# Retention and a SwiGLU layer on one core: the sums of weight blocks are made in other units, kept in DRAM and read back for every unit

## The chip, the cores and the metric

The kernel runs on one core of a Trainium2 chip. The metric is the device time of one execution, in microseconds (us); lower is better. The kernel before took 670.7 us, the median of three runs (670.59 to 671.23).

The engines are named as in the profile: PE (TensorE, matmuls) with PEld (its weight loads), DVE (VectorE), ACT (ScalarE), POOL (GpSimd) and SP (SyncE, which here only issues DMAs). SBUF is the memory that the engines work on, PSUM the one that matmuls write to, DRAM the memory off the core.

## The reference: what is computed

Two layers, one after the other. The first is retention with a decay per head, in blocks of 64; the second is a SwiGLU layer after an RMS norm:

```python
intra = einsum('bhic,bhjc->bhij', qb, kb) * Dmask          # per block of 64
out[:, :, sl] = einsum('bhij,bhjd->bhid', intra, vb) + einsum('bhid,bhde->bhie', qb * lam_pow, kv_state)
kv_state = lam_block * kv_state + einsum('bhsd,bhse->bhde', kb * rev_pow, vb)

xn = x / sqrt(mean(x * x) + 1e-6) * rms_g                  # x: 3072 tokens x 512
g, val = xn @ w_gate, xn @ w_val                           # 512 x 1536 each
result = (g / (1 + exp(-g)) * val) @ w_out                 # 1536 x 512
```

Batch 4, 8 heads, 768 positions, head size 64: 3072 tokens of width 512. Everything is float32 at the kernel's borders.

## The kernel before

**Tiling.** The tokens are cut into six groups m = 0 to 5 of 512, the hidden width 1536 into twelve slices f = 0 to 11 of 128. A unit is one pair (m, f): the gate and the value product of that slice, the activation, and its share of the output product. There are 72 units, in the order m=0 with f=0..5, m=1 with f=0..11, m=0 with f=6..11 (units 0 to 23), and then m=2 to 5 with twelve slices each (units 24 to 71). Between the units run the retention products of a later group, as pairs of heads (`Pair`), and that group's norm (`Norm`).

**Precision.** Every operand of the large products is held as a float16 high part and a float16 rest (for the output product of the early units, as two parts in another 32-bit format). A product takes three passes: high by high, rest by high, high by rest.

**Two kinds of units.** Units 0 to 23 are classical: 12 matmuls of 128x512 for the gate, 12 for the value, 12 for the output. Units 24 to 71 (`strassen`) replace the eight half-size block products of gate and value by seven (`Product`, numbered 1 to 7), each of six 128x256 matmuls (L939). Products 3, 5, 6 and 7 read sums of weight blocks, and 5 to 7 sums of token blocks (`tx`) as their other operand. The output product takes 12 matmuls of 128x512 (L777 to L779).

**The sums of weight blocks** (`WeightSums`, one per slice f). The high part and rest of both weights are first added up (`whole`, two steps on POOL, L871); four steps on DVE form the four sums (`sums`, L886 to L890); each is then split into its float16 parts by copies on ACT (`high`, L904) and differences on POOL (`low`, L908). Where the result lies is told by `place`: the first two sums in the spare half of the tile of an output weight (`w16`), the third in memory that held the weights' squares (`col`) or a partial result (`partial`), the fourth over half of the gate weight of that slice itself. The last two can be written only when their places are no longer read. The sums of f = 0, 1 and 2 are due in units 18 to 20, those of 3 to 11 from unit 24.5 on, one per unit.

**Other work around them.** The weights arrive as raw 64-bit words on SP's queue and are converted in units up to 14 (`Weights`; TAKE). `Column` forms squares of each weight for bounds that unit 17 needs (`Norms`). `Halves` turns the output weights into float16 pairs once these bounds are known: f = 6 to 11 from unit 18.35 on, f = 0 to 5 from 24.5 on; each takes two steps on ACT (L268, L274), one on DVE (L277) and one on POOL (L282), with two of the three buffers of the tag "o". The same buffers serve the squares and the rows of the result.

**The order of the work.** Units 0 to 5 (`ramp`) are written out by hand. From unit 6 on, a planner (`Plan`) orders all steps: each has an engine, a cost in us, a due time in units, tiles that it reads and writes, and buffers that it opens. The planner walks through time, takes for each engine the step with the earliest due time that can start, and emits the instructions in that order. On the chip each engine then keeps this order. Loads of q, k and v ("LD"), of output weights ("LO") and stores ("ST") are engines of their own to the planner, but all of them go into the one queue of SP, which is served in order. A product step writes its PSUM bank: the "ps" tile for even units (`pp`), "pg" and "pv" for odd ones (`pa`, `pb`). A norm's factors (`spread`, `pr`, L658) take the "ps" tile too in m = 2 and 3.

## Time and profile before

| what | value |
|---|---|
| median of three runs | 670.7 us (670.59 to 671.23) |
| the profiled execution's own time | 672.56 us |
| its span, first to last instruction | 670.8 us |
| PE busy | 652.3 us, 97% |
| DVE busy | 428.0 us, 64% |
| ACT busy | 328.9 us, 49% |
| POOL busy | 160.1 us, 24% |
| DRAM traffic | 44.05 MB read, 6.29 MB written |
| granted TensorE clock | 0.998 |

How to read it: a row of waits names the instruction that stood idle, what released it, the total in us, the number of times and the longest. A row of lines gives line, engine, operation, tiles (out<-in), shapes, count, then busy us and the mean in ns, then the idle time ahead of it. A row of the timeline begins with the start in us from the span's beginning and the length in us; idle time ahead of it stands in brackets.

### The profile page before, as it was taken

The page shows a single profiled execution, that of the slowest core. Times are in us where ns is not written, and L with a number is a line of the kernel's source. Part 1 is how long each engine was busy: PE and PEld are TensorE (multiplying, and loading weights), DVE is VectorE, ACT ScalarE, POOL GpSimd, SP SyncE. Part 2 cuts the span into 40 slices and gives each one's busy share as a digit, 9 for nine tenths or more (in the row PEclk, how much of TensorE's full clock was granted, in tenths as well). Part 3 has the DMA queues.
Part 4 walks back from the last instruction along what each step waited for, and adds up shares of the span by engine and source line. Part 5 has one row for each costly group of instructions (what it writes and reads, how often), then busy time and mean ns, then how long its engine had stood idle before and what let it go on. Part 6 is the DMA issues. An engine that isn't in the chain of part 4 may idle for free.

```text
span 670.8 us, 12331 instructions
## 1 busy us (share of the span) xinstructions
PE 652.3 (97%) x5035; PEld 442.9 (66%) x5035; DVE 428.0 (64%) x779; ACT 328.9 (49%) x672; POOL 160.1 (24%) x144
## 2 busy tenths in 40 slices
PE   8999999999999999999979999999999999999997
PEld 8846665555656446777657777777777776767774
DVE  6798869876346887987875434477644377543333
ACT  3786558675324644564454443335444434433332
POOL 2300130012205844868822011001111001000000
PEclk9999999999999999999999999999999999999999
DMA  8966626311023001301100321100220000100001
GB/s 313 345 237 213 232 75 233 114 63 64 0 64 127 1 0 55 128 29 44 64 1 1 110 79 64 64 1 2 95 96 1 1 1 1 39 26 1 1 1 63
DMA packets 14312, 51.12 MB, mean 76 GB/s; under 512 B 1712, under 2 KB 1968, under 8 KB 12848
## 3 DMA queue, kind: packets, MB, share of 16 engines
q1 hardware_dynamic: 13968, 49.69, 20.9%
q8 instruction: 39, 0.64, 0.4%
q10 hardware_dynamic: 288, 0.66, 0.3%
q14 instruction: 17, 0.14, 0.1%
HBM read 44.05 MB, written 6.29 MB: 75 GB/s over the span
## 4 chain that ended last, share of the span: by engine, by line
PE 86%; DVE 8%; ACT 2%; POOL 1%; issue 1%; DMA 0%; DVEq 0%; ACTq 0%; POOLq 0%
PE pp L939 16%; PE pv L758 9%; PE acc L777 9%; PE pg L758 9%; PE pa L939 8%; PE acc L779 8%; PE acc L778 8%; PE pb L939 6%; PE pa L508 4%; PE po L569 3%; PE po L580 2%; PE pst L537 2%; DVE tx L990 1%; DVE ws L887 1%; ACT tx L986 1%
## 5 line engine op out<-in xcount | busy, mean ns | idle before, releaser
L779 PE MATMUL acc<-wo,hh 128*128 128x512 f16 (+1 forms) x288 | 110.3, 383 | 0.0
L778 PE MATMUL acc<-wo,hh 128*128 128x512 f16 (+1 forms) x288 | 110.2, 383 | 0.0
L777 PE MATMUL acc<-wo,hh 128*128 128x512 f16 x216 | 82.3, 381 | 0.2 <-DVE hh L1035 0.2
L939 PEld LDWEIGHTS <-wo 128*128 128x128 f16 x576 | 55.8, 98 | 30.1 <-issue 8.1
L939 PEld LDWEIGHTS <-wg 128*128 128x128 f16 x576 | 56.3, 98 | 19.4 <-issue 4.4
L758 PE MATMUL pg<-x,wg 128*128 128x512 f16 x288 | 67.8, 380 | 0.8 <-ACT sg L1010 0.5
L1028 ACT CAST hh<-sg 128x512 f16<-128x512 f32 (+1 forms) x72 | 44.4, 617 | 48.4 <-DVE sg L1017 23.5
L758 PE MATMUL pv<-x,wv 128*128 128x512 f16 x288 | 67.0, 379 | 0.0
L986 ACT COPY tx<-pp 128x256 f32<-128x256 f32 x72 | 26.8, 372 | 78.7 <-PE pp L939 76.3
L939 PEld LDWEIGHTS <-wv 128*128 128x128 f16 x576 | 56.2, 98 | 9.3 <-DVE xn L731 1.2
L528 POOL TENSOR_TENSOR qkv<-qkv,pw 128x512 f32<-128x512 f32 x22 | 28.4, 1291 | 106.2 <-PE pa L508 97.3
L990 DVE TENSOR_TENSOR tx<-pp,tx 128x256 f32<-128x256 f32 x48 | 20.3, 423 | 51.7 <-ACT sg L998 40.0
L986 ACT COPY tx<-pa 128x256 f32<-128x256 f32 x72 | 26.7, 371 | 48.7 <-PE pa L939 48.0
L758 PEld LDWEIGHTS <-wv 128*128 128x128 f16 x288 | 27.9, 98 | 33.6 <-issue 1.1
L758 PEld LDWEIGHTS <-wg 128*128 128x128 f16 x288 | 26.5, 98 | 34.7 <-issue 5.2
L1035 DVE TENSOR_TENSOR hh<-sg,hh 128x512 f16<-128x512 f32 x54 | 43.2, 800 | 5.1 <-ACT hh L1028 4.2
L939 PE MATMUL pp<-tx,wo 128*128 128x256 f16 x288 | 39.0, 272 | 3.9 <-DVE tx L990 3.1
L1004 DVE SCALAR_TENSOR_TENSOR sg<-tx,cv,sg 128x512 f32<-128x512 f32 x48 | 39.6, 825 | 4.1 <-DVE tx L990 0.5
L994 DVE TENSOR_TENSOR sg<-pp,tx 128x256 f32<-128x256 f32 x24 | 10.1, 423 | 45.5 <-ACT tx L986 43.5
L939 PE MATMUL pp<-x,wg 128*128 128x256 f16 x288 | 35.5, 272 | 3.1 <-DVE sg L994 2.6
L990 DVE TENSOR_TENSOR tx<-pb,tx 128x256 f32<-128x256 f32 x48 | 20.3, 424 | 27.9 <-PE pb L939 25.1
L779 PEld LDWEIGHTS <-hh 128*128 128x128 f16 x216 | 21.1, 98 | 25.5
(192 smaller groups left out, 1270.4 us busy)
## 6 DMA issues: line engine op xcount, KB each, us to landing
qkv<-in_qkv_dram SPq DMA_DIRECT2D x47, 512.0 KB, 4.8
raw_gv<-in_weights_dram SPq DMA_DIRECT2D x11, 1024.0 KB, 5.3
raw_o<-in_weights_dram SPq DMA_DIRECT2D x12, 512.0 KB, 4.4
out_dram<-o SPq DMA_DIRECT2D x23, 256.0 KB, 2.1
partial<-in_weights_dram SPq DMA_DIRECT2D x2, 512.0 KB, 11.4
qkv<-in_qkv_dram ACTq DMA_DIRECT2D x1, 512.0 KB, 4.0
out_dram<-o SPq DMA_DIRECT2D x1, 128.0 KB, 1.7
out_dram<-o ACTq DMA_DIRECT2D x1, 128.0 KB, 2.4
```

The costliest lines, as they stand in the source:

```text
L508: nc.tensor.matmul(self.pa[:, j, c, :], self.kT[r, c, :], self.qT[r, c, :], start=True, stop=True,)
L528: eng.tensor_mul(self.qT, self.qT, pw[:, p : p + 1, :].broadcast_to([P, GC, P]))
L758: nc.tensor.matmul(ps, w[:, kk, :], x[:, kk, :], start=i == kk == 0, stop=i == 2 and kk == NK - 1,)
L777: nc.tensor.matmul(acc, hl[:, ts_], oh, start=first, stop=False)
L778: nc.tensor.matmul(acc, hh[:, ts_], ol, start=False, stop=False)
L779: nc.tensor.matmul(acc, hh[:, ts_], oh, start=False, stop=last)
L939: nc.tensor.matmul(ps, w(ow, k), x(ox, k), start=first and i == k == 0, stop=i == 2 and k == 1, skip_group_check=True,)
L986: nc.scalar.copy(self.kept[:, i], self.pa)
L990: nc.vector.tensor_add(self.val[:, half], self.pb, self.kept[:, i])
L1004: nc.vector.scalar_tensor_tensor(self.sg, self.val, cv[:, self.f : self.f + 1], self.sg, ALU.mult, ALU.mult)
L1028: nc.scalar.copy(self.hh, self.sg)
L1035: nc.vector.tensor_sub(self.hl, self.sg, hh)
```

## The change

The sums of weight blocks no longer stay in SBUF. Each sum's float16 parts are formed in two buffers of the tag "o" and stored to DRAM as two blocks of 256 KB (`put`). Each of the units 24 to 71 reads the whole set of its slice back, 512 KB, into one of three buffers (`fetch`), the former places of output weights 8, 9 and 11, taken in turn. The fourth sum is read from there too, and no longer overwrites the gate weight.

Because no place has to become free, the sums of f = 0 to 5 can be made as soon as the weights are there: they are now due from unit 12.5 to 16.25, those of 6 to 11 from 24.8 to 30.3. A sum's splitting takes two copies on ACT and two differences on POOL, all of 128x512, instead of three each. The float16 output weights are put two to a tile (`PLACE`). The squares of the weights (`column_steps`) are due one unit earlier.

The planner has a fourth queue to order ("FE", the fetches, again on SP), adds 0.8 of the overlap to the cost of eight named kinds of DVE steps while POOL is busy (before: a quarter to every DVE step), looks 600 steps ahead instead of 420, and gets markers ("turn:...") that keep the users of the PSUM banks in the order of the units.

```diff
 class Halves: def high(self):
-            place = {HALF: NF, 0: NF - 1}.get(f, f - 1)
-            self.t = t = wpool.tile([P, 4, DM], F16, tag=f"wo{place}", name=f"wo16_{f}")
+            if f % 2 == 0:
+                w16[f] = w16[f + 1] = wpool.tile(
+                    [P, 2, 2, DM], F16, tag=f"wo{PLACE[f]}", name=f"wo16_{f}"
+                )
+            self.t = t = w16[f][:, f % 2]
...
+    PLACE = {6: 12, 8: 6, 10: 7, 0: 10, 2: 0, 4: 1}
+    STREAM = [8, 9, 11]
...
 class WeightSums:
+                self.t = stage.tile(
+                    [P, 2, 2, HG], F32, tag="raw_o", name=f"ws_{self.f}", bufs=2
+                )
             t = self.t
             if i == 0:
-                nc.vector.tensor_add(t[:, 0], g0, g1)
-                nc.vector.tensor_sub(t[:, 2], v0, g0)
+                nc.vector.tensor_add(t[:, 0, 0], g0, g1)
+                nc.vector.tensor_sub(t[:, 0, 1], v0, g0)
             else:
-                nc.vector.tensor_sub(t[:, 1], g1, t[:, 2])
-                nc.vector.tensor_sub(t[:, 3], v1, t[:, 1])
...
+                nc.vector.tensor_sub(t[:, 1, 0], g1, t[:, 0, 1])
+                nc.vector.tensor_sub(t[:, 1, 1], v1, t[:, 1, 0])
+
+        def high(self, i):
+            if i == 0:
+                self.o = {}
+            self.o[i] = o = op.tile([P, 2, 2, HG], F16, tag="o", name=f"s_{self.f}_{i}")
+            nc.scalar.copy(o[:, 0], self.t[:, i])
+
+        def low(self, i):
+            nc.gpsimd.tensor_sub(self.o[i][:, 1], self.t[:, i], self.o[i][:, 0])
+
+        def put(self, i):
             f = self.f
             if i == 0:
+                sums_dram[f] = dram.tile([P, 2, 2, 2, HG], F16, tag=f"sd{f}", name=f"sd_{f}")
+            nc.sync.dma_start(sums_dram[f][:, i], self.o[i])
+
+    def fetch(u, f):
+
+        t = wpool.tile(
+            [P, 2, 2, 2, HG], F16, tag=f"wo{STREAM[u % 3]}", name=f"ss_{u}"
+        )
+        nc.sync.dma_start(t, sums_dram[f])
+        streamed[u] = t
...
 class Product:
-                (raw(wg, 0), given(2, second)),
+                (summed(1, 1), given(2, second)),
                 (raw(wg, 2), given(0, second)),
-                (lambda o, k: pairs12[f][:, o, 0, cols[k]], lambda o, k: t[:, o, k, 0]),
-                (lambda o, k: pairs12[f][:, o, 1, cols[k]], lambda o, k: t[:, o, k, 1]),
-                (lambda o, k: s3[:, o, cols[k]], lambda o, k: t[:, o, k, 2]),
+                (summed(0, 0), lambda o, k: t[:, o, k, 0]),
+                (summed(1, 0), lambda o, k: t[:, o, k, 1]),
+                (summed(0, 1), lambda o, k: t[:, o, k, 2]),
...
 class Plan:
+        SHARED = (
+            "low", "mul_sums", "sums", "refine", "rest_high", "convert", "convert_o", "add_squares",
+        )
-        ENGINES = ("PE", "ACT", "DVE", "POOL", "LD", "LO", "ST")
+        ENGINES = ("PE", "ACT", "DVE", "POOL", "LD", "LO", "ST", "FE")
-        def run(self, horizon=1.3, reach=420):
+        def run(self, horizon=1.3, reach=600):
-                if eng == "DVE" and start < pool_until:
-                    cost *= 1.25
+                if eng == "DVE" and fn.__name__ in self.SHARED and start < pool_until:
+                    cost += 0.8 * min(cost, pool_until - start)
...
 def sum_steps(f, at):
+            step("POOL", 1.15, at + 0.1 * i, s.whole, i, r=[f"w{'vg'[i]}{f}"], w=[f"r{f}:{i}"],
+                 new=[] if i else [(f"r{f}", "a")])
         for i in range(2):
+            step("DVE", 0.84, at + 0.4 + 0.1 * i, s.sums, i, r=[f"r{f}:0", f"r{f}:1"], w=[f"ws{f}:{i}"],
+                 new=[] if i else [(f"ws{f}", "raw_o")])
+        for i in range(2):
+            step("ACT", 0.62, at + 0.6 + 0.1 * i, s.high, i, r=[f"ws{f}:{i}"], w=[f"so{f}{i}"],
+                 new=[(f"so{f}{i}", "o")])
+            step("POOL", 1.15, at + 0.7 + 0.1 * i, s.low, i, r=[f"ws{f}:{i}"], w=[f"so{f}{i}"])
+            step("ST", 0.05, at, s.put, i, r=[f"so{f}{i}"], w=[f"sd{f}:{i}"], lasts=4.0)
+
+    def fetch_steps(u, f):
+        step("FE", 1.5, 0, fetch, u, f, r=[f"sd{f}:0", f"sd{f}:1"], w=[f"ss{u}"],
+             new=[(f"ss{u}", f"wo{STREAM[u % 3]}")], lasts=4.0)
...
 def classical(u, h, norms=None):
-            w = [f"{name}{u}"]
+            w = [f"{name}{u}", f"turn:{name}"]
...
-                w.append("pc")
+                w += ["pc", "turn:pa"]
...
 def strassen(u, h):
+        fetch_steps(u, f)
+        s = f"ss{u}"
-        step("PE", cost, u, h.first, u, r=[v, *x01], w=[a], new=banks)
+        step("PE", cost, u, h.first, u, r=[v, *x01], w=[a, "turn:pg", "turn:pv"], new=banks)
...
-        step("PE", cost, u + 0.8, h.add, 3, r=[g, *x23], w=[b])
+        step("PE", cost, u + 0.8, h.add, 3, r=[s, *x23], w=[b])
...
-    SUMS = [(18, 18.6), (19, 19.6), (20, 20.3)]
-    SUMS += [(2 * NF, 2 * NF + 0.5 + 1.0 * (f - 3)) for f in range(3, NF)]
+    SUMS = [(12 if f < 5 else 16, 12.5 + 0.75 * f if f < 6 else 24.8 + 1.1 * (f - 6)) for f in range(NF)]
...
-                column_steps(f, u + 0.3)
+                column_steps(f, u - 0.7)
```

## The prediction

> **What bounds the kernel now.** I read the page first, then who TensorE (PE) waited for in stretches between unit ends, then the load of the other engines there.

> ```profile
> span 670.8 us, 12331 instructions
> ...
> PE 652.3 (97%) x5035; PEld 442.9 (66%) x5035; DVE 428.0 (64%) x779; ACT 328.9 (49%) x672; POOL 160.1 (24%) x144
> ...
> PE 86%; DVE 8%; ACT 2%; POOL 1%; issue 1%; DMA 0%; DVEq 0%; ACTq 0%; POOLq 0%
> ```

> PE is busy for 97% of the span and holds 86% of the chain that ended last. The change leaves the number of matmuls alone, so it can only win time in which PE stands still. The page puts that at 18.5 us (670.8 - 652.3), but it understates each stall, because a matmul's modelled end overlaps the next one:

> ```profile
> 595.73 0.38 PE L778 MATMUL acc<-wo,hh 128*128 128x512 f16 x1
> 595.95 0.38 PE L779 MATMUL acc<-wo,hh 128*128 128x512 f16 x1
> ```

> Starts are 0.22 apart and the recorded length is 0.38, so every listed wait hides another 0.16 us or so. Below, a stall costs its listed idle time plus 0.16.

> Group 2 (the twelve units of m=2, from the end of unit 23 at 254.5 to the end of unit 35 at 369) is where the waits gather. The waits of PE from 254 to 325, then from 325 to 369:

> ```profile
> PE pp L939 <- DVE sg L994: 1.8, 3, 0.7
> PE pp L939 <- DVE tx L990: 0.3, 1, 0.3
> PE pa L939 <- ACT tx L986: 0.2, 1, 0.2
> ```

> ```profile
> PE pp L939 <- ACT tx L986: 2.0, 3, 1.0
> PE pp L939 <- DVE xn L731: 0.9, 1, 0.9
> PE pp L939 <- DVE sg L994: 0.8, 2, 0.6
> PE pr L658 <- POOL y L649: 0.5, 1, 0.5
> ```

> First part: 2.3 + 5 x 0.16 = 3.1 us. Second part: 4.2 + 7 x 0.16 = 5.3 us. Together 8.4. The next group does the same products and the same kind of attention work with no weight sums, and loses 0.7 + 2 x 0.16 = 1.0 us in all (waits of PE from 369 to 471):

> ```profile
> PE pp L939 <- DVE tx L990: 0.7, 2, 0.3
> ```

> So about 7 us is the price of what group 2 does beside its products: nine of the twelve weight sums, and six of the twelve halvings of the output weights. The load of the engines in units 12 to 16, the two parts of group 2, and group 3 (columns: PE, PEld, DVE, ACT, POOL busy, clock, DMA share, GB/s):

> ```profile
> 138.70:179.00 40.30, 40.30 (x199) 22.25 (x198) 22.99 (x46) 21.95 (x40) 4.85 (x7) 1.00 0.08 28
> ...
> 254.50:325.00 70.50, 68.30 (x630) 49.09 (x627) 58.70 (x92) 38.33 (x86) 49.66 (x43) 1.00 0.23 76
> 325.00:369.00 44.00, 39.79 (x308) 28.43 (x306) 31.66 (x56) 21.52 (x49) 18.68 (x17) 1.00 0.01 1
> 369.00:470.80 101.80, 101.15 (x873) 73.40 (x872) 55.51 (x105) 43.83 (x96) 11.12 (x9) 1.00 0.15 53
> ```

> VectorE (DVE) is 83% busy in the first part and 55% in group 3; GpSimd (POOL) 70% against 11%. They are also in each other's way. The first three rows are DVE's sums from 254.5 to 325; the last is the same step over the whole kernel (min/median/max ns):

> ```profile
> L887 DVE TENSOR_TENSOR ws<-r 128x256 f32<-128x256 f32 x6 | 8.7, 1451 | 0.0
> ...
> L890 DVE TENSOR_TENSOR ws<-r,ws 128x256 f32<-128x256 f32 x6 | 5.2, 864 | 0.2
> L886 DVE TENSOR_TENSOR ws<-r 128x256 f32<-128x256 f32 x6 | 4.6, 767 | 1.3 <-POOL wg L908 1.2
> ...
> L889 DVE TENSOR_TENSOR ws<-r,ws 128x256 f32<-128x256 f32 x6 | 3.2, 536 | 0.0
> ```

> ```profile
> L887 DVE TENSOR_TENSOR ws<-r x12: 412/1372/1495, 196.0 to 354.0; 128x256 f32<-128x256 f32 x12
> ```

> One 128x256 step takes 0.41 us alone and up to 1.5 us beside GpSimd's; a sum's four cost 3.6 us (1.45 + 0.86 + 0.77 + 0.54) where 4 x 0.41 = 1.65 would do. The last sum's steps ran at 354, 15 us before the group's end: the sums trail through all of it.

> **The change part by part.**

> *PE's work: 0.* Seven products of six matmuls read the same shapes from another tile.

> *Sums 3 to 5 leave group 2, 6 to 11 stay (due 24.8 to 30.3).* In the first part six sums ran before (L887 x6) and six will run after. Per sum DVE has the same four steps; GpSimd has two halves of 512 instead of one of 512 and two of 256:

> ```profile
> L871 POOL TENSOR_TENSOR r<-wv 128x512 f32<-128x512 f16 x7 | 8.9, 1266 | 4.9 <-DVE ws L890 3.8 <-PE po L569 1.2
> L871 POOL TENSOR_TENSOR r<-wg 128x512 f32<-128x512 f16 x6 | 8.4, 1393 | 0.0
> ...
> L908 POOL TENSOR_TENSOR wo<-ws,wo 128x512 f16<-128x512 f32 x6 | 7.6, 1271 | 1.5 <-ACT wo L904 1.5
> L908 POOL TENSOR_TENSOR wg<-ws,wg 128x256 f16<-128x256 f32 x6 | 5.8, 969 | 0.2 <-ACT wg L904 0.2
> ```

> That is 1.27 + 1.39 + 1.27 + 2 x 0.97 = 5.9 us before and 1.27 + 1.39 + 2 x 1.27 = 5.2 after, too little to matter. So I leave the 3.1 us of the first part as they are (bounds: all of it gone, or 3.1 more). The second part loses its three sums. What stalls there is the norm of m=3 (unit 31): its spread sits in the PSUM bank that unit 32 needs until DVE has read it four times, the last read ending just before PE goes on:

> ```profile
> 336.34 0.74 DVE L731 SCALAR_TENSOR_TENSOR xn<-x,gs,pr 128x512 f32<-128x512 f32 x1
> ```

> ```profile
> 337.14 1.49 PE L939 MATMUL pp<-x,wv 128*128 128x256 f16 x12 [0.88 <-DVE xn L731]
> ```

> and then unit 32 runs alone, step by step, because the output products that would fill its gaps wait for DVE too. With DVE and GpSimd free of sums this should shrink to what the worst of the other hand-offs between groups costs, that before m=5 (waits of PE from 574 to 604):

> ```profile
> PE pp L939 <- DVE tx L990: 0.6, 2, 0.3
> PE pp L939 <- DVE x L719: 0.4, 1, 0.4
> PE pp L939 <- ACT tx L986: 0.3, 1, 0.3
> ```

> 1.3 + 4 x 0.16 = 1.9 us. So 5.3 - 1.9 = **3.4 us won** (bounds 0 and 5.3).

> *Sums 0 to 2 leave units 18 to 22.* There PE lost one stall, to the norm of m=2, and the sum of weight 2 is straight ahead of it on DVE:

> ```profile
> 232.17 0.43 DVE L890 TENSOR_TENSOR ws<-r,ws 128x256 f32<-128x256 f32 x1
> 232.51 0.68 DVE L609 TENSOR_TENSOR sq<-sq,sq 128x512 f32<-128x512 f32 x1
> ```

> ```profile
> PE pss L625 <- DVE sq L609: 0.8, 1, 0.8
> ```

> **1.0 us won** (0.8 + 0.16; bounds 0 and 1.0).

> *Sums 0 to 5 come into units 12 to 16.* PE is full there without a single wait, GpSimd is used for 4.9 of 40.3 us, DVE for 23.0. Six sums add 9.9 us to DVE at the step's lone time and 21.7 at the time beside GpSimd: 33 to 45 of 40.3. A unit there asks only two DVE steps of PE's path (gating and the low half), and both have the 12 gate matmuls (2.6 us at 0.22) before their bank is wanted. I take 0, the lower bound, because the nearest row is that of three sums in the equally classical units 18 to 21, which cost PE nothing but the norm's stall. The upper bound is the first part's 3.1 us, or 4.4 where DVE is overfull (45 - 40.3, rounded down; a rival below).

> [...]

> *The column work (square sums of the weights) moves one unit earlier:* into units 7 to 15, same steps; hidden behind PE's matmuls as before, 0. If that cover is gone it is the same rival.

> *24 stores and 48 loads are added on SyncE's queue.* A store is 256 KB and a load 512 KB in 4 KB rows; the nearest rows are the result's stores and the output weights' loads, with the latter's landing times min/median/max:

> ```profile
> out_dram<-o SPq DMA_DIRECT2D x23, 256.0 KB, 2.1
> ```

> ```profile
> DMA to landing us min/median/max: 3.6/4.4/9.4
> ```

> A load for unit u+3 is free to go after unit u's last use of its buffer, two units ahead. Two units take 14.8 us:

> ```profile
> 603.21 0.62 ACT L1028 CAST hh<-sg 128x512 f16<-128x512 f32 x1
> ```

> ```profile
> 618.05 0.62 ACT L1028 CAST hh<-sg 128x512 f16<-128x512 f32 x1
> ```

> Even the slowest landing, 9.4, leaves 5 us: 0 (upper bound below, as a rival). Traffic: 512 KB per 7.4 us is 71 GB/s above the 53 to 76 of the stretches above. A store waits for GpSimd's low half, and what stands behind it on the queue are q/k/v loads, the results' stores and the next loads of sums. A stall of a few us there is covered by the same 14.8 us; sums 6 to 11 are due about five units before their use.

> *Halvings keep their four instructions and only change place.* 0. They share three buffers with the stored sums, which now hold two of them until a store has landed. At 1.27 for the low half and 2.1 for the landing, six sums hold 6 x 2 x 3.4 = 41 of the 211 buffer-us (3 x 70.5) of the first part, so a halving rarely finds none.

> *The planner's new costs, turns and reach* change the order of everything after the ramp. It can add or take single stalls of 0.5 us: 0, plus or minus 1.5.

> **Sum:** -3.4 - 1.0 = -4.4 us. The profiled execution took 672.56 us, 1.76 around its span, so it would take 668.2. The median of the runs shown is 670.70, 1.86 below it; carried over, 666.3.

> **Rivals.**

> *Sums were DVE's whole trouble.* The sums' lower GpSimd load and a better order also clear the first part: 3.1 more, and the hand-off costs nothing: 1.9 more. 661.3. For it: group 3 loses only 1.0. Against: six sums and the halvings still run in that part, as densely as now.

> *The hand-off is the norm's own.* The bank is held by four reads in DVE's order whatever else runs; then only the 1.0 us goes: 669.7, no change. For it: three of its waits are on ScalarE copies in a chain inside one unit. Against: the hand-offs to m=4 and m=5 are cheap; but these norms take another way.

> *DVE overfull in units 12 to 16 (slower).* If a sum there costs DVE over 2.9 us ((40.3 - 23.0) / 6), weight 11 and the column sums come late and PE stands at unit 17, which needs both: 4.4 us. The same contention keeps sums 6 to 11 trailing into the norm of m=3, so that the 3.4 isn't won: 670.7 + 4.4 - 1.0 = 674.1. For it: the median of 1.37 us; against: the deadline is unit 17, and DVE has room in units 16 and 17.

> *A load of sums stuck behind a q/k/v load.* SyncE takes its queue in order, and it has stood on such loads for long:

> ```profile
> SPq L86 <- PE po L580: 228.9, 11, 53.2
> ```

> Nothing waited behind them before; now a load of sums may. The mean wait is 20.8 us, the cover 14.8 - 4.4 = 10.4, so each case costs 10.4: one of them, 676.7. Against: the planner issues both in the order in which their buffers come free.

> **How the numbers follow.** Forecast 0.48 (its own range 662.9 to 667.8: the hand-off at nothing instead of 1.9, and the planner's 1.5 either way); everything cleared 0.14; hand-off unchanged 0.14; DVE overfull 0.18; stuck load 0.06. The predicted time is the forecast's, 666.3. The range runs from 661.3 to 674.3: below it little is left to win, above it lie the stuck load and a part of the overfull case, under 2 in 10. A change under 0.2% (1.3 us) can't be told from none here: faster 0.62, same 0.14, slower 0.24.

> **What would show it.** Right: PE waits after 325 fall to about 2 us, the wait on L609 is gone, the first part keeps about 3 us of waits, units 12 to 17 have none, and no PE row is released by a DMA. Wrong: a wait of unit 17's first products on DVE or on the columns' bank; PE rows that end with the landing of a sum's load; the norm of m=3 still releasing unit 32 late although GpSimd is idle; or the DVE steps of sums 0 to 5 near 0.4 us and yet new stalls, which would put the loss in the planner's order.

## The result, and the profile after

The changed kernel takes **674.39 us** in the median against 670.7 us, a ratio of **1.0052** (95% interval 1.0034 to 1.0069): 0.5% slower, where 666.3 us and faster was forecast. One execution of each kernel is left out (836.18 us at a granted clock of 0.754 after, 1704.07 us before), and the profile after is that of a further execution at full clock (673.3 us of span, 675.03 us of its own time; that of before: 670.8 and 672.56).

The page of the changed kernel, its busy times and the shares of the chain that ended last:

```profile
span 673.3 us, 12464 instructions
...
PE 652.6 (97%) x5035; PEld 443.2 (66%) x5035; DVE 432.8 (64%) x779; ACT 327.7 (49%) x660; POOL 164.0 (24%) x132
...
PE 61%; DVE 7%; ACT 2%; POOL 1%; issue 1%; DVEq 0%; ACTq 0%
```

PE's work is the same (652.6 after, 652.3 before). The chain can be followed back only to 187 us here, so its shares add up to 72% and can't be set beside the 86% of before; from there on no DMA is in it, and no wait of PE in the whole profile is released by one. So the 2.5 us between the two spans are again time in which PE stands. Line numbers have moved by a few: gate and value products L764, block products L941, output products L783 to L785, the cast of the hidden values L1031, their low half L1038, the gating L1020, the sums' steps L880 to L884, the store of a sum L899, the read of one L906.

The waits of PE from 138 to 195 us (units 12 to 17), where before had none at all (row: engine, line, what released it, total us, times, longest):

```profile
PE acc L783 <- DVE hl L1038: 1.8, 1, 1.8
PE pst L543 <- ACT sg L1013: 0.9, 1, 0.9
PE pn L455 <- ACT junk L450: 0.7, 1, 0.7
PE pv L764 <- DVE sg L1020: 0.3, 1, 0.3
PE pc L338 <- DVE a L530: 0.2, 1, 0.2
```

In the order of the rows, PE waits for the low half of the hidden values, for a state product's PSUM bank that ScalarE must first have read (`pst`), for the sums of a norm, for the gating and for an attention step. By the prediction's rule (listed wait plus 0.16) that is 3.9 + 5 x 0.16 = **4.7 us that were not there before**. From 195 to 255 us the list of PE's waits is empty: the stall on the norm of m=2 is gone. From 254 to 325:

```profile
PE pp L941 <- DVE sg L997: 1.8, 3, 0.8
PE pp L941 <- DVE tx L993: 1.0, 3, 0.6
PE pa L514 <- DVE tx L993: 0.3, 1, 0.3
PE pa L941 <- ACT tx L989: 0.2, 1, 0.2
```

3.3 + 8 x 0.16 = 4.6 us, against 3.1 before. From 325 to 369:

```profile
PE pp L941 <- DVE tx L993: 0.6, 1, 0.6
PE pp L941 <- ACT tx L989: 0.3, 1, 0.3
PE pr L664 <- POOL y L655: 0.2, 1, 0.2
```

1.1 + 3 x 0.16 = 1.6 us, against 5.3. So: +4.7 - 1.0 + 1.5 - 3.7 = +1.5 us in the stretches that the prediction spoke of. The load of the engines in the first two stretches, in the columns of before:

```profile
138.70:179.00 40.30, 39.27 (x179) 21.94 (x178) 38.68 (x61) 23.96 (x45) 26.63 (x21) 1.00 0.26 92
179.00:254.50 75.50, 72.67 (x526) 41.51 (x525) 46.40 (x89) 33.11 (x58) 31.77 (x25) 1.00 0.24 84
```

The first row is the one to look at: VectorE went from 22.99 to 38.68 of 40.3 us, GpSimd from 4.85 to 26.63. How that becomes a stall of PE shows in VectorE's timeline ahead of the longest wait:

```profile
180.74 0.68 DVE L300 TENSOR_REDUCE ts<-wo 128x1 f32<-128x512 f32 x1
181.34 1.00 DVE L317 TENSOR_TENSOR sq_w<-sq_w 128x512 bf16<-128x512 bf16 x1
182.26 1.37 DVE L880 TENSOR_TENSOR ws<-r 128x256 f32<-128x256 f32 x1
183.56 0.89 DVE L881 TENSOR_TENSOR ws<-r 128x256 f32<-128x256 f32 x1
184.49 0.42 DVE L883 TENSOR_TENSOR ws<-r,ws 128x256 f32<-128x256 f32 x1
184.94 0.42 DVE L884 TENSOR_TENSOR ws<-r,ws 128x256 f32<-128x256 f32 x1
185.29 0.74 DVE L1020 SCALAR_TENSOR_TENSOR sg<-pv,cg,sg 128x512 f32<-128x512 f32 x1
...
187.05 1.01 DVE L1038 TENSOR_TENSOR hl<-sg,hh 128x512 fp32r<-128x512 f32 x1 [0.51 <-ACT hh L1031]
```

The rows of PE that it feeds and that wait for it:

```profile
177.86 2.75 PE L764 MATMUL pv<-x,wv 128*128 128x512 f16 x12 [0.34 <-DVE sg L1020]
...
188.12 0.50 PE L783 MATMUL acc<-wo,hl 128*128 128x512 f32 x1 [1.76 <-DVE hl L1038]
```

The value product was complete at 180.6 (177.86 + 2.75); it was gated (L1020) at 185.29, behind a reduction, a square sum and a whole weight sum. The gating's other operand, ScalarE's `sg`, was ready at 182.11, so 3.2 us of this delay are VectorE's queue alone. The rest goes with the sums too: ScalarE made that operand right behind a copy of a sum's high part (L890), which began at 180.90, when VectorE had finished the sum at 180.82. The cast and the low half follow, and PE waits for that low half until 188.12. From 180.74 until after the gating VectorE has no gap; it is the order and the length of what stands in its queue.

What happens after group 2 doesn't matter to the result: the cast that ends unit 35 starts at 369.01 before and at 371.55 after, and the last matmul at 666.02 and 668.47, so 2.5 us later both times. The 48 reads cost nothing. The issues of DMAs (KB each, median us to landing), and the landing of the reads:

```profile
ss<-sd SPq DMA_DIRECT2D x48, 512.0 KB, 3.3
...
sd<-s SPq DMA_DIRECT2D x24, 256.0 KB, 2.0
...
DMA to landing us min/median/max: 3.2/3.3/4.8
```

Most of the remaining microsecond lies ahead of the planner's part. The cast of the hidden values, first and last start, before and after:

```profile
L1028 ACT CAST hh<-sg x72: 605/618/628, 48.3 to 662.2; 128x512 f16<-128x512 f32 x54, 128x512 fp32r<-128x512 f32 x18
```

```profile
L1031 ACT CAST hh<-sg x72: 600/618/628, 49.0 to 664.7; 128x512 f16<-128x512 f32 x54, 128x512 fp32r<-128x512 f32 x18
```

From the first cast to the last it is 613.9 us before and 615.7 after, and 615.9 in a further profile of the changed kernel (48.0 to 663.9): **from there on the change costs 1.8 to 2.0 us**. The first cast moves between executions although the units up to it are written out by hand and the same in all (more on this at the end).

### The profile page after: what moved, and what is told of

Read it like the earlier page. It is cut to its first block, busy times and chain, and to the rows that moved or that the text cites. A ratio compares the mean times of both kernels' runs of the same rounds, so it can differ in the third digit from the quotient of the medians.

```text
span 834.4 us, 12464 instructions
## 1 busy us (share of the span) xinstructions
PE 825.1 (99%) x5035; PEld 506.5 (61%) x5035; DVE 424.5 (51%) x779; ACT 328.4 (39%) x660; POOL 160.6 (19%) x132
## 4 chain that ended last, share of the span: by engine, by line
PE 97%; DVE 1%; ACT 1%; DMA 0%; issue 0%; ACTq 0%; DVEq 0%
PE pp L941 17%; PE pg L764 10%; PE pv L764 10%; PE acc L783 10%; PE pa L941 10%; PE acc L784 9%; PE acc L785 9%; PE pb L941 7%; PE pa L514 4%; PE po L575 4%; PE po L586 3%; PE pst L543 2%; PE pss L631 1%; DVE tx L993 1%; PE unread L147 1%; PE pr L664 1%
## 5 line engine op out<-in xcount | busy, mean ns | idle before, releaser
L941 PEld LDWEIGHTS <-ss 128*128 128x128 f16 x1152 | 128.0, 112 | 62.3 <-issue 33.3
L785 PE MATMUL acc<-wo,hh 128*128 128x512 f16 (+1 forms) x288 | 133.1, 462 | 0.0
L784 PE MATMUL acc<-wo,hh 128*128 128x512 f16 (+1 forms) x288 | 133.0, 462 | 0.0
L783 PE MATMUL acc<-wo,hh 128*128 128x512 f16 x216 | 97.3, 450 | 0.0
L764 PE MATMUL pg<-x,wg 128*128 128x512 f16 x288 | 86.4, 459 | 0.0
L764 PE MATMUL pv<-x,wv 128*128 128x512 f16 x288 | 86.3, 459 | 0.0
L941 PEld LDWEIGHTS <-wv 128*128 128x128 f16 x576 | 65.5, 114 | 18.0 <-DVE xn L737 1.3
L941 PE MATMUL pp<-tx,ss 128*128 128x256 f16 x432 | 69.0, 315 | 1.8 <-DVE tx L993 0.6
L1031 ACT CAST hh<-sg 128x512 f16<-128x512 f32 (+1 forms) x72 | 44.5, 618 | 63.8 <-DVE sg L1020 35.3
L764 PEld LDWEIGHTS <-wv 128*128 128x128 f16 x288 | 31.9, 112 | 47.6 <-issue 45.0
L764 PEld LDWEIGHTS <-wg 128*128 128x128 f16 x288 | 30.5, 113 | 47.6 <-issue 43.1
L941 PE MATMUL pa<-tx,ss 128*128 128x256 f16 x288 | 49.4, 319 | 0.0
L941 PE MATMUL pp<-x,wv 128*128 128x256 f16 x288 | 45.6, 321 | 0.6 <-DVE xn L737 0.6
L785 PEld LDWEIGHTS <-hh 128*128 128x128 f16 x216 | 24.2, 112 | 35.1 <-issue 30.9
L941 PEld LDWEIGHTS <-wg 128*128 128x128 f16 x288 | 33.1, 115 | 20.4 <-issue 14.8
L1038 DVE TENSOR_TENSOR hh<-sg,hh 128x512 f16<-128x512 f32 x54 | 41.3, 766 | 5.3 <-ACT hh L1031 4.5
## 6 DMA issues: line engine op xcount, KB each, us to landing
sd<-s SPq DMA_DIRECT2D x24, 256.0 KB, 2.0
out_dram<-o SPq DMA_DIRECT2D x23, 256.0 KB, 2.2
```

The lines of the kernel that those rows point to most:

```text
L764: nc.tensor.matmul(ps, w[:, kk, :], x[:, kk, :], start=i == kk == 0, stop=i == 2 and kk == NK - 1,)
L783: nc.tensor.matmul(acc, hl[:, ts_], oh, start=first, stop=False)
L784: nc.tensor.matmul(acc, hh[:, ts_], ol, start=False, stop=False)
L785: nc.tensor.matmul(acc, hh[:, ts_], oh, start=False, stop=last)
L941: nc.tensor.matmul(ps, w(ow, k), x(ox, k), start=first and i == k == 0, stop=i == 2 and k == 1, skip_group_check=True,)
L1031: nc.scalar.copy(self.hh, self.sg)
```

## The experiments

Each stretch below is priced as above, from the list of PE's waits. The edits are against the changed kernel where nothing else is said.

| kernel | median us | ratio (95%) | 138-195 | 195-254 | 254-325 | 325-369 |
|---|---|---|---|---|---|---|
| before | 670.7 | | 0 | 1.0 | 3.1 | 5.3 |
| after | 674.8 | 1.0052 (1.0036 to 1.0069) | 4.7 | 0 | 4.6 | 1.6 |
| after, a third time | 673.5 | 1.0031 (1.0018 to 1.0044) | 4.9 | 0 | 4.6 | 1.6 |
| planner alone | 668.7 | 0.9969 (0.9960 to 0.9979) | 0 | 0 | 1.8 | 5.5 |
| old cost rule | 675.4 | 1.0056 (1.0036 to 1.0076) | 2.3 | 0 | 7.8 | 1.6 |
| columns back | 672.0 | 1.0012 (0.9999 to 1.0026) | 3.0 | 0 | 4.6 | 1.6 |
| first six later | 668.9 | 0.9958 (0.9944 to 0.9972) | 0 | 0.9 | 4.2 | 1.6 |
| without GpSimd's part | 668.5 | 0.9962 (0.9947 to 0.9976) | 0 | 0 | 4.6 | 1.6 |
| all before unit 24 | 679.6 | 1.0108 (1.0073 to 1.0143) | 3.2 | 0.8 | 7.0 | 1.2 |
| last six later too | 674.1 | 1.0052 (1.0036 to 1.0069) | 0 | 0.9 | 7.7 | 3.5 |
| eight before | 674.3 | 1.0046 (1.0029 to 1.0063) | 0 | 0.9 | 9.2 | 1.2 |
| first six later, own buffer | 668.4 | 0.9970 (0.9958 to 0.9981) | 0 | 0 | 3.1 | 3.0 |
| eight before, own buffer | 677.7 | 1.0102 (1.0087 to 1.0117) | 0 | 0.8 | 11.0 | 1.2 |
| six in own buffer | 669.2 | 0.9981 (0.9969 to 0.9993) | 0 | 0 | 3.2 | 3.5 |

The columns count idle time alone. In six of these profiles the granted clock also fell to 0.50 after a stall (last section), which the columns don't contain: for about 3.4 us once with the planner alone, the old cost rule, the columns back and eight before; for about 6.8 us with eight before in their own buffer; and for 3.4 and 6.8 us with all before unit 24. By estimate from the matmuls' spacing (0.43 us where 0.23 is usual, last section) that costs half of the time, 1.7 us for each 3.4. With it the rows come near the measured times: eight before in its own buffer has 13.0 us of waits against 9.4 before, and 3.6 + 3.4 = 7.0 us is what its median lost (677.67 against 670.76).

**The changed kernel again.** No edit.

> The changed kernel as it is, for a profile at the full clock. Theory A (the forecast's gain is there, but eaten elsewhere): PE waits from unit 32 on (the former 5.3 us) are about 2 us, and some 8 us of new waits stand in units 6 to 31. Theory B (the planner's new order loses it): no part of group 2 is better, waits on DVE and ACT steps of the units themselves. Theory C (fetches): PE rows that end with a landing of ss, at least 4 us in all. Theory D (clock): the waits of PE fall by some 4 us as forecast, and the span is longer all the same, with a granted clock below that of before.

674.76 us, 1.0052 again; its profile is the one shown above.

**The planner alone.** The kernel before with the planner's part of the change and nothing else: sums stay where they were, in SBUF.

```diff
+        SHARED = ("low", "mul_sums", "sums", "refine", "rest_high", "convert", "convert_o", "add_squares")
-        def run(self, horizon=1.3, reach=420):
+        def run(self, horizon=1.3, reach=600):
-                if eng == "DVE" and start < pool_until:
-                    cost *= 1.25
+                if eng == "DVE" and fn.__name__ in self.SHARED and start < pool_until:
+                    cost += 0.8 * min(cost, pool_until - start)
...
+        (the markers "turn:..." of the PSUM banks)
```

> The kernel before with the planner's changes alone (the overlap cost of eight kinds of DVE steps, 600 steps of reach, the turn markers); sums, places and due times as before. Theory B: slower than before by 3 to 8 us. Theories A, C and D: within 1.5 us of before (669.2 to 672.2).

668.66 us, 0.9969: the planner's part wins 2 us by itself. The wait of 195 to 255 is gone although sums 0 to 2 are still made there, and the first part of group 2 falls to 1.8. The second part stays, with the norm of m=3 as its longest wait:

```profile
PE pp L939 <- DVE xn L731: 2.4, 1, 2.4
```

So the 1.0 us that I gave to the sums' leaving can be had by the order alone, and the 3.7 of the second part isn't won by it. That the sums' leaving alone wins them isn't shown either. Ahead of the wait above, VectorE runs from 327.18 to 332.03 without a gap on steps of the norm, its token sums and one gating, at 0.42 and 0.74 to 0.75 us each; none of them is a sum, and none is stretched. And two kernels below, with no sum left in the second part (own buffer), lose 3.0 and 3.5 us there.

**The old cost rule.** The change with the planner's former rule for VectorE.

```diff
-                if eng == "DVE" and fn.__name__ in self.SHARED and start < pool_until:
-                    cost += 0.8 * min(cost, pool_until - start)
+                if eng == "DVE" and start < pool_until:
+                    cost *= 1.25
```

> The changed kernel with the planner's former cost rule (a quarter on every DVE step beside GpSimd) in place of the new one. Theory B: faster than the changed kernel by 3 us or more, back near 670.7. Theories A, C, D: within 1.5 us of the changed kernel.

675.38 us, 1.0056: the same time as after, by another way. Units 12 to 17 lose 2.3 instead of 4.7, the first part of group 2 7.8 instead of 4.6. The cost rule is worth 3.2 us in the dense part of group 2 and pays 2.4 of it in units 12 to 17.

**The columns back.** The square sums of the weights due where they were.

```diff
-                column_steps(f, u - 0.7)
+                column_steps(f, u + 0.3)
```

> The changed kernel with the weights' squares due one unit later, as before. If the early squares crowd DVE and ACT in units 7 to 12 (a form of theory A): 1 to 4 us faster than the changed kernel, with PE waits gone between 100 and 145 us. Otherwise within 1 us of it.

671.95 us, 1.0012. Two of the five waits of units 12 to 17 stay:

```profile
PE pst L543 <- ACT sg L1013: 1.8, 1, 1.8
PE pv L764 <- DVE sg L1020: 0.9, 1, 0.9
```

2.7 + 2 x 0.16 = 3.0. So the column work's move, which I costed at nothing, has a share of 1.7 us of the waits, in a place where VectorE is full; the rest stays with the sums. In this profile the wait at 178 was also followed by a halved clock (below), which hides about 1.7 us of the gain.

**The first six sums later.** Sums 0 to 5 due from unit 17 to 21.5 instead of 12.5 to 16.25; 6 to 11 stay.

```diff
-    SUMS = [(12 if f < 5 else 16, 12.5 + 0.75 * f if f < 6 else 24.8 + 1.1 * (f - 6)) for f in range(NF)]
+    SUMS = [(17, 17.0 + 0.9 * f) if f < 6 else (17, 24.8 + 1.1 * (f - 6)) for f in range(NF)]
```

> The changed kernel with the sums of f = 0 to 5 due at 17.0 + 0.9 f instead of 12.5 + 0.75 f; all else as changed. Theory A (units 12 to 16 are overfull on DVE): DVE's load from 138.7 to 179 falls from 38.7 back to about 23 us, PE's lost time from 138 to 195 from 5.7 to about 1.2 us, and the kernel is about 4 us faster than the changed one. Theory B (it is the new order of the whole, not this place): the 4 us stay, wherever they then stand.

668.85 us, **0.9958: faster than both kernels**, 0.4% below the one and, by the two ratios, 0.7 to 0.9% below the other. The waits of units 12 to 17 are gone and those of the other stretches hardly differ from after. VectorE's load where it was full, in the columns of before:

```profile
138.70:179.00 40.30, 40.30 (x204) 22.43 (x203) 26.33 (x52) 22.39 (x41) 11.10 (x12) 1.00 0.13 49
179.00:254.50 75.50, 74.76 (x529) 42.09 (x528) 55.08 (x95) 33.36 (x59) 44.73 (x35) 1.00 0.27 98
```

26.33 instead of 38.68 us, with PE full. In units 17 to 23, where these sums now stand, VectorE takes 55.08 of 75.5 us, and loses PE only 0.9. So the loss belongs to sums 0 to 5 in units 12 to 16, and the store and the read-back are not to blame. Against the planner alone (668.66 us, 0.9969) this kernel is no clear gain: the two intervals overlap, so no run here shows that keeping the sums in DRAM is worth anything beyond the planner's part.

**Without GpSimd's part.** Sums 0 to 5 in the changed kernel's places, but the two GpSimd steps of each half are left out: the sums are formed on VectorE from the weights' high parts alone, and the high part is stored twice. These sums have no rests, so this is less work and another sum.

```diff
         def whole(self, i):
+            if self.f < 6: return
...
+            if self.f < 6:
+                r2 = [w[:, self.f, 0] for w in (wv, wg)]
...
         def low(self, i):
+            if self.f < 6: return
```

> The changed kernel in its own order with GpSimd's 24 steps of the sums of f = 0 to 5 left out (the sums are formed from the high parts alone and stored twice, so the result is less exact). DVE and ACT keep all their steps. If DVE is late because it waits beside GpSimd: DVE's load from 138.7 to 179 falls from 38.7 to about 31 us, its 24 steps of these sums go to 0.42 us each, PE's lost time from 138 to 195 falls from 5.7 to under 2 us. If the number of DVE steps is too much in itself: 4 us or more stay.

668.5 us, 0.9962, and no wait of PE from 138 to 195, though VectorE still makes five sums there:

```profile
138.70:179.00 40.30, 40.30 (x204) 22.45 (x203) 31.35 (x67) 26.92 (x50) 7.87 (x7) 1.00 0.29 100
```

The same sums and places, 31.35 us of VectorE in place of 38.68 (for 67 steps in place of 61), GpSimd 7.87 in place of 26.63, and the waits of the later stretches as after. What overfills VectorE is therefore the time that its steps lose beside GpSimd's. It is not waiting for GpSimd's results: VectorE was idle for only 1.6 of the 40.3 us after. The sums read float16 here and float32 after, but the short ones of after take 0.41 to 0.42 us as well. The groups of VectorE's lines from 138.7 to 179, after:

```profile
L1038 DVE TENSOR_TENSOR hl<-sg,hh 128x512 fp32r<-128x512 f32 x5 | 5.4, 1073 | 0.8 <-ACT hh L1031 0.8
...
L880 DVE TENSOR_TENSOR ws<-r 128x256 f32<-128x256 f32 x4 | 4.0, 998 | 0.0
...
L881 DVE TENSOR_TENSOR ws<-r 128x256 f32<-128x256 f32 x4 | 2.6, 654 | 0.0
L884 DVE TENSOR_TENSOR ws<-r,ws 128x256 f32<-128x256 f32 x3 | 2.5, 823 | 0.1
...
L883 DVE TENSOR_TENSOR ws<-r,ws 128x256 f32<-128x256 f32 x3 | 1.2, 412 | 0.0
```

A sum costs 1.00 + 0.65 + 0.41 + 0.82 = 2.9 us, and the low half that PE waits for costs 1.07 in the mean, against 0.69 in the kernel without GpSimd's part. The same step takes 0.41 us or up to 1.49 (L881, the whole changed kernel), and without GpSimd's part the four steps of a sum take 0.42 to 0.51 us in the mean. The runs show these durations, not in what way the two engines delay each other.

**All sums before unit 24.** All twelve due from unit 14.5 to 23.85, columns as before.

```diff
+    SUMS = [(14, 14.5 + 0.85 * f) for f in range(NF)]
-                column_steps(f, u - 0.7)
+                column_steps(f, u + 0.3)
```

> All twelve sums due before unit 24 (14.5 + 0.85 f), the weights' squares at their former time. Theory A: group 2 without sums loses about 1.5 us from 258 to 326 (changed kernel: 4.6) and about 1.8 from 326 to 372, units 12 to 17 about 1.2, so 665 to 668 us. If the halvings and the attention alone crowd the first part: 4.6 stays there, 669 to 671.

679.64 us, 1.0108, the slowest, and far above both times that I had expected. Units 12 to 17 lose 3.2 and the first part of group 2 loses 7.0 although only two sums are still made in it; the lowered clock behind the two longest stalls adds about 5.1 by the estimate above.

**The last six later too.** As the first six later, and sums 6 to 11 due from unit 26.0 on instead of 24.8.

```diff
+    SUMS = [(17, 17.0 + 0.9 * f) if f < 6 else (17, 26.0 + 1.0 * (f - 6)) for f in range(NF)]
```

> As the run with the sums of f = 0 to 5 due from 17.0 on, and those of f = 6 to 11 due at 26.0 + 1.0 (f - 6) instead of 24.8 + 1.1 (f - 6). If the first part of group 2 loses its 4.4 us because the first sums meet the halvings and the hand-off into that group: the stalls of 264 to 273 (2.6 us) go and the time falls to 666 to 668. If it is only the planner's order around them: they stand elsewhere, and the time stays at 668 to 670.

674.05 us, 1.0052, against 666 to 670 expected: the gain of the first six is given back, 3.5 us of it in the first part and 1.9 in the second. It is also the one kernel in which a read of sums released PE:

```profile
PE pp L941 <- DMA ss<-sd: 0.4, 1, 0.4
```

**Eight before, four after.** Sums 0 to 7 due from 17.0 on, 8 to 11 from 26.0.

```diff
+    SUMS = [(17, 17.0 + 0.75 * f) if f < 8 else (17, 26.0 + 1.2 * (f - 8)) for f in range(NF)]
```

> As that run, with eight sums due from 17.0 to 22.25 and four at 26.0 + 1.2 (f - 8). If DVE's load in group 2 is what counts: PE loses under 2.5 us from 258 to 326 and the time is 666 to 668. If units 17 to 23 have no room for two more sums: new stalls of 2 us or more between 200 and 262, and 669 to 672.

674.32 us, 1.0046, again above both expectations. The second part falls to 1.2, and the first rises to 9.2, half of it (1.3 and 3.6 us) in two stalls at 258 to 264, where the units go over to group 2.

**The parts in a buffer of their own.** Three kernels in which a sum's float16 parts go into one 4 KB buffer of the converter's tag "w" and no longer share "o" with the halvings: with the first six later (all sums, and only f under 6), and with eight before.

```diff
-            self.o[i] = o = op.tile([P, 2, 2, HG], F16, tag="o", name=f"s_{self.f}_{i}")
+            if i == 0:
+                self.both = cvt.tile([P, 2, 2, 2, HG], F16, tag="w", name=f"s_{self.f}")
+            self.o[i] = o = self.both[:, i]
```

> As the run with the sums of f = 0 to 5 due from 17.0 on, but the float16 parts of all sums are formed in the one buffer of the tag w (4 KB) instead of two of the three buffers of the tag o. If the parts that wait for their stores keep the halvings from their buffers, and that is what group 2's first part pays for: it loses under 2.5 us from 258 to 326 instead of 4.4, and the time falls to 666 to 667.5. If it is DVE's order: 4 us or more stay there, 668 to 671.

> The same change of buffer on the run with eight sums due before unit 23, which lost 9.8 us from 258 to 326 with one stall of 3.6 us on a halving. If the buffers are the cause: that stall goes and the time falls by 3.5 us or more, to 671 or less. If not: within 2 us of 674.3.

> As the first, but only the sums of f = 0 to 5 use the buffer w, those of 6 to 11 keep the buffers o. If the buffers count: it lies between 668.85 and the first. If DVE's order counts: 668 to 671, no nearer to either.

668.42, 677.67 and 669.2 us. If the shared buffers made the first part's stalls, the middle one should have won most. Its twin's stall on a halving did go, but a longer one came in its place, and it lost 3.4 us against the twin (677.67 to 674.32). With the first six later, the first part falls from 4.2 to 3.1 and 3.2 us and the second rises from 1.6 to 3.0 and 3.5; the time hardly moves (668.42 and 669.2 against 668.85). So the shared buffers don't set the time; since each edit also makes the planner order the steps anew, these runs can't tell more. What the longest stall of the middle kernel shows is the norm of m=2 run late: PE's wait in the first part, and VectorE just ahead of it:

```profile
PE po L575 <- DVE a L530: 4.4, 2, 3.8
```

```profile
256.68 1.40 DVE L737 SCALAR_TENSOR_TENSOR yt<-x,gs,pr 128x512 f32<-128x512 f32 x2
258.00 0.74 DVE L737 SCALAR_TENSOR_TENSOR hy<-x,gs,pr 128x512 f32<-128x512 f32 x1
...
260.37 1.49 DVE L748 TENSOR_TENSOR xt<-yt 128x256 f32<-128x256 f32 x1
...
262.57 1.22 DVE L530 TENSOR_TENSOR a<-pa,mask 128x1024 f32<-128x1024 f32 x1
```

VectorE is still at the norm and the token sums of m=2 when group 2 begins, and the attention step `a` that PE needs stands behind them. The stretch before it:

```profile
179.00:254.50 75.50, 74.90 (x519) 41.98 (x518) 58.06 (x91) 33.04 (x59) 50.17 (x39) 1.00 0.30 107
```

VectorE was 58.06 us busy in this kernel and GpSimd 50.17, against 46.40 and 31.77 after, and against 55.08 and 44.73 with the first six later, which lost only 0.9 us there. VectorE isn't full over this stretch as it was in units 12 to 16; that the additional sums push the norm back is the reading that fits, and no run tests it by itself.

**The changed kernel a third time.** No edit; the question is when the ramp ends.

> The changed kernel once more, for a second profile at the full clock. PE loses the same 18 to 20 us in the same places; if the landing of the first load of constants (3.9 us in the first such profile, 2.4 in three others) decides part of the time, the ramp's end moves with it, by some 2 us between the profiles.

673.52 us, 1.0031. The load of the first constants landed 2.4 us after its issue, as in four kernels with an early first cast (2.2 to 2.4), and yet the first cast came at 48.0; with the first six later it landed in 3.0 us and the cast came at 46.4. The landing doesn't decide it.

**Gaps of set length.** With the first six later, 4, 6, 8 and 10 more VectorE steps of 0.42 us ahead of the gate sums of units 62, 64, 66 and 68, to see from which stall on the clock drops: 682.65 us in a single execution.

```diff
+            for _ in range({62: 4, 64: 6, 66: 8, 68: 10}.get(self.u, 0)):
+                nc.vector.tensor_add(self.sg[:, :HG], self.kept[:, 0], self.kept[:, 0])
```

> The kernel with the sums of f = 0 to 5 due from 17.0 on, with 4, 6, 8 and 10 additional DVE steps of 0.42 us ahead of the gate sums of units 62, 64, 66 and 68, to make PE stand still for rising times in a stretch that is otherwise regular. If a standstill of about 2 us halves the granted clock for 3.4 us afterwards, as in four profiles: the shorter gaps leave the clock at 1.0, those of 2 us and more are each followed by one stretch at 0.5, worth another 1.7 us. If those four were chance: no such pattern.

PE's rows behind the last three gaps, and the stretches from there on (the third number from the end of a row is the granted clock):

```profile
608.42 0.83 PE L941 MATMUL pp<-x,wg 128*128 128x256 f16 x6 [2.32 <-DVE sg L999]
...
626.67 0.83 PE L941 MATMUL pp<-x,wg 128*128 128x256 f16 x6 [3.23 <-DVE sg L999]
...
645.83 1.46 PE L941 MATMUL pp<-x,wg 128*128 128x256 f16 x6 [4.16 <-DVE sg L999]
```

```profile
608.00:611.40 3.40, 2.98 (x26) 2.55 (x27) 1.28 (x4) 1.36 (x3) 0.00 (x0) 1.00 0.14 25
626.70:630.00 3.30, 3.30 (x28) 2.68 (x29) 1.18 (x2) 1.31 (x4) 0.00 (x0) 1.00 0.23 55
645.00:648.50 3.50, 2.67 (x13) 1.92 (x14) 0.76 (x2) 0.51 (x1) 0.00 (x0) 0.52 0.00 0
```

Idle time of 2.32 and 3.23 us left the clock at 1.00, 4.16 halved it: a single length of about 2 us as the threshold, which I had expected, is refuted.

## Why the prediction was wrong

**The step that failed** is "Sums 0 to 5 come into units 12 to 16: I take 0, the lower bound". Measured: 4.7 us, within a few tenths of the upper bound of 4.4 that stood beside it. I chose between the two ends by the nearest row, three sums in units 18 to 21, but there three sums were spread over four units (VectorE 49.99 us busy of the 75.5 from 179 to 254.5, before), and here six go into five units that also convert weights. The working had the numbers for the other end: 23.0 + 21.7 of 40.3 us. Leaving out GpSimd's part, or making the six later, removes the loss completely, so it is shown that these sums beside GpSimd cause it. Of the 5.9 us between the forecast -4.4 and the +1.5 found in the waits, 4.7 are this step and 1.5 the first part of group 2.

*The cover was misread.* I set the 12 gate matmuls (2.6 us) against "two VectorE steps of PE's path". The steps are short, but VectorE keeps its order, and what stands ahead of them counts: the gating at 185.29 ran 4.7 us after its product was ready, and 3.2 us after its other operand. A cover has to be compared with the queue ahead of a step, not with the step.

*The columns one unit earlier* (0): not nothing. Putting them back takes 1.7 us of waits away, in the place that VectorE's overload made tight.

*The second part of group 2* (3.4 won): the size is right, 3.7; it keeps 1.6 where 1.9 was said. The reason is shown only in part: the kernel with the planner alone, which still makes sums there, keeps 5.5, but kernels without sums there keep from 1.2 to 3.5, so the order counts as well.

*Sums 0 to 2 leave units 18 to 22* (1.0 won): the size is right, the reason isn't needed. With the sums still there the planner's new order clears the same stall.

*The first part* (stays at 3.1): 4.6, inside its bounds. The planner alone brings it to 1.8; with the new places of the sums it lies between 3.1 and 11.0, and not by the number of sums in it: with two made there it lost 7.0, with seven 1.8. Which step of the order decides in each case stays open. A buffer of their own for the sums' parts doesn't remove the loss. In the kernels with eight or twelve sums ahead of unit 24 the norm of m=2 stands late in VectorE's queue at the longest stall, in two of the three together with a halving.

*Stores, loads and halvings* (0): right. From the end of unit 35 to the end both kernels take the same time, landings have a maximum of 4.8 us against the 9.4 that I allowed for, and the changed kernel has no PE row released by a DMA.

*The median carried over from the profile* (-1.86): before's profiled execution happened to be one of its longer ones (672.56; in another set 5 of its 21 executions lay at 672.4 to 673.1, the rest at 670.4 to 671.3). The profiles shown of the changed kernel lie only 0.3 and 0.8 us above their medians. Its executions lie in two groups as well (third time: five at 672.6 to 673.1, five at 673.9 to 674.9), but more often in the upper one. So of the 3.7 us between the medians about 2 are seen in the profiles, group against group too, and the rest is that the changed kernel falls more often into its upper group; why it does is open.

*The rivals.* "DVE overfull in units 12 to 16" named the right engine, stretch and price: its 2.9 us per sum is what a sum took. Its second half was wrong, since the 3.4 us of the second part were won all the same; and PE stood from 164 to 189 us on gating, norms and low halves, with only 0.2 us on the columns' bank. That its 674.1 fits the median is luck: by the waits the time would be 670.7 + 1.5 = 672.2, and the two microseconds that no wait explains fill the gap. "Sums were DVE's whole trouble" fell with the first part, "the hand-off is the norm's own" fell with the second for the changed kernel, though with the planner alone the norm's own steps do hold PE up for 2.4 us, and the stuck load wasn't seen.

## What to carry to other kernels

Work moved to an engine that looks half free has to be priced at the duration that it has beside the engine it will run with, not alone, and the sum set against that stretch: here a sum took 2.9 us of VectorE beside GpSimd's steps and 1.8 with those left out (there without its rests), and 45 of 40.3 us stood in the working and was set aside. The slack of a step on the critical path has to be counted behind the whole queue ahead of it on its engine: here the gating ran 3.2 us after its last operand was ready. When a change moves work and alters the planner too, run the planner alone: here it was worth 0.3% by itself, and the whole change is faster than before (0.9958) only with the first six sums due from unit 17 on, where the engine has room for them, and then not clearly faster than the planner alone (0.9969).

## What the runs showed of the hardware

```profile
181.00:184.40 3.40, 3.40 (x10) 2.70 (x9) 3.06 (x7) 3.17 (x7) 3.40 (x3) 0.50 0.31 119
```

The output matmuls there start 0.43 us apart where 0.23 is usual, so by estimate such a stretch costs 1.7 us. It was also seen after a stall of 2.36 us at the norm of m=3 (planner alone, 0.50 from 333.1 to 336.5), of 2.31 us (all before unit 24, from 186.2 to 189.7; 0.83 in the mean of 180 to 190), of 3.40 us (eight before, 0.50 from 263.6 to 267.0) and of 1.97 us between float16 products (old cost rule, from 317.5 to 321.0; 0.97 in the mean of 258 to 326). After 3.83 and 4.36 us it lasted some 6.8 us (eight before in its own buffer, from 263.0; 0.95 in the mean of 254.5 to 325; and all before unit 24, from 264.7; 0.74 in the mean of 260 to 270 and 0.92 of 270 to 280). It was not seen after 1.76 us at 188 in the changed kernel (1.00 from 179 to 254.5), nor after 2.32 and 3.23 us with the gaps of set length (1.00 in both stretches). So between 1.8 and 3.2 us the length alone doesn't tell: 2.31 and 2.36 us halved the clock, 2.32 us didn't. What decides there isn't settled by these runs. The kind of products around the stall isn't enough: between float16 products 1.97 us halved the clock and 3.23 us didn't.

**The ramp is not the same in each execution.** In fifteen profiles at full clock with the same hand-written units 0 to 5 the first cast starts between 46.2 and 49.0 us: in nine from 46.2 to 47.0 (46.4 with the first six later, 46.6 with the planner alone), in six from 48.0 to 49.0 (48.3 before, 49.0 and 48.0 in the changed kernel). That is up to 2.8 us, more than the change is worth. The landing of the first load doesn't decide it (3.0 and 3.1 us in three of the nine, 2.4 in one of the six). The profiles of the kernel before and both of the changed one are among the six; the cause stays open.
